# Opening input transposes cut into 128x32 column tiles, bias sums moved behind them over 128 rows, and rows 0-255 put first on SyncE's queue

## The chip, the cores and the metric

The kernel runs on one core of a Trainium2 chip. A core has five engines that work side by side and meet through semaphores: TensorE (PE in the profile), VectorE (DVE), ScalarE (ACT), GpSimd (POOL) and SyncE (SP). SP issues nothing but transfers here; ACT and POOL issue some as well, each in the order of its own instructions. The metric is the device time of one execution in microseconds, and the time of a kernel is the median of its runs.

## The reference

Six cross layers, each a product with a 416x416 matrix, a bias, a product with the first input, and a residual:

```python
B, F, D, L = 4096, 26, 16, 6
Din = min(F * D, 1024)          # 416

def reference(x0, ws, bs):      # (4096,416), (6,416,416), (6,416), all bf16
    x = x0
    for l in range(ws.shape[0]):
        x = x0 * (x @ ws[l] + bs[l]) + x
    return x
```

Since x starts as x0, the residual is folded away: the kernel keeps the running sum of `x @ ws` in PSUM, and adds to it the running sum of the biases plus 1. What a layer stores is x0 times that. So the bias is needed once, as six prefix sums for each of the 416 features.

## The kernel before

**Tiling.** The 4096 rows are four blocks of 1024 (`s`), each of two halves of 512. Features lie on partitions: three chunks of 128 (`c`, `k`, `m`) and a tail of 32. For each block and layer (`n = s * L + l`, 24 in all) TensorE does, in this order: half 0 of the three main chunks (`chunk`, `step`, 36 matmuls, each group of four filling the four column tiles of the array), the products with the 32-feature tail (`row`, L393 and L409, in two parts), the tail's own output (128x32 tiles with 256 columns), and half 1. All matmuls written through `tile_mm` are recorded at L265, whatever they compute.

**The others, in a layer.** DVE turns each PSUM chunk into the next layer's input (L537), ACT and POOL handle the tail (L595, L242, L566). TensorE waits for them by `s_xa`, `s_xb` and `s_sw`.

**The opening.** Before the first layer can run, x0 must have features on partitions. Its first block comes in four pieces of 256 rows. Piece 0 (`xin_sb[:, 0:2]`), piece 1 (`[:, 2:4]`) and piece 2 (`[:, 4:6]`) are loaded row by row and transposed by TensorE; piece 3 is transposed by a DMA (L158) that SP issues when piece 0 has landed.

- Transfers: SP issues biases (L134), piece 0 (L135), piece 2 (L136). ACT issues piece 1 (L137), the first layer's weights (L138), the tail of piece 3 (L139), then two small weight loads (L125), and only then loads its activation table.
- TensorE, in order: 40 warm-up matmuls on constants (L130, ten rounds of four column tiles); the bias sums (16 tiny matmuls over the 7 rows of `bsa_sb`, one row of ones and six of biases, against a triangle of ones `u_sb`); one more round on constants (`fill`); twelve 128x128 transposes of pieces 1 and 0 (L312) in `IN_ORDER`, whose pairs are (piece, chunk); then layer 0. In layer 0 the loop over `k` is outside: `k` 0, 1 and 2, three rounds of four matmuls each. Ahead of each `k` stands `before_a(k)`, a wait for the transposed inputs of that chunk.
- Before the second round of `k` 2 come `tail_inputs` (16 matmuls against the identity, for the tail) and `third_input` (24 of the same, for piece 2, into fp32 PSUM).
- DVE copies the bias sums out of PSUM (L506), then chunks 0 and 2 of pieces 1 and 0 (L512), later chunks 0 and 2 of piece 2 (L517). ACT copies chunk 1 (L561 and L578) and the tail (L576).

The order is written out by hand; what ties it together is the semaphores (`s_inT` counts transposed chunks, `s_inD` and `s_inA` the copies of DVE and ACT). PSUM has 8 banks. Bank 1 holds the bias sums; pieces 1 and 0 use banks 0, 5, 7 and 3, 4, 6 (`IN_BANKS[h]`); the tail uses bank 5; piece 2 uses banks 3, 6, 7.

Of the kernel before, what the change touches and what calls it, by code (L numbers as in the profile page):

```python
# [11 lines left out]
def bass_standalone__dcn_v2_cross__recsys_kernel(  # L12
# [20 lines left out]
    with ExitStack() as es:  # L33
# [20 lines left out]
        o_sb = sb("o_sb", [128, NJ, D])  # L54
        ident = sb("ident", [128, 128])
        ones_sb = sb("ones_sb", [128, 256])
        bsa_sb = sb("bsa_sb", [L + 1, D])
        u_sb = sb("u_sb", [L + 1, L])
        cb_sb = sb("cb_sb", [128, NC + 1, L], FP32)
        cq_sb = sb("cq_sb", [128, NC + 2], FP32)  # L60
        ps = es.enter_context(nc.psum_tensor("ps", [128, 8, 512], FP32))
# [34 lines left out]


        IN_BANKS = ((3, 4, 6), (0, 5, 7))
        IN_ORDER = ((1, 0), (1, 1), (1, 2), (0, 0), (0, 1), (0, 2))
        THIRD = (3, 6, 7)  # L100

        NAT_BANKS = (0, 1, 2, 6, 7, 4, 3, 5)
# [2 lines left out]
        def lane(g):  # L105
            return slice(32 * g, 32 * g + 32)
# [19 lines left out]
                wt_sb[lane(g), a:b, 0:n1 - n0], ws[a:b, DF:D, n0:n1].rearrange("l p n -> p l n")  # L126
            ).then_inc(done, 16)

        for q in range(4 * 10):
            nc.tensor.matmul(  # L130
                ps[lane(q % 4), 7, 0:256], lhsT=CONST[:, 0:32], rhs=CONST, start=True, stop=True,
                skip_group_check=True, tile_position=(0, 32 * (q % 4)),
            )
        nc.sync.dma_start(bsa_sb[1:L + 1, :], bs[:, :]).then_inc(s_bs, 16)  # L134
        nc.sync.dma_start(xin_sb[:, 0:2, :], x0_w[:, 0, :, :]).then_inc(s_xin[0], 16)  # L135
        nc.sync.dma_start(xin_sb[:, 4:6, :], x0_w[:, 2, :, :]).then_inc(s_xin[2], 16)  # L136
        nc.scalar.dma_start(xin_sb[:, 2:4, :], x0_w[:, 1, :, :]).then_inc(s_xin[1], 16)  # L137
        nc.scalar.dma_start(w_sb[:, 0, :, :], wmain(0)).then_inc(s_w[0], 16)  # L138
        nc.scalar.dma_start(xtl_sb[:, :, :], x0_v[:, 6:JS, DF:D]).then_inc(s_xtl0, 16)  # L139
        nc.gpsimd.memset(ones_sb[:, :], 1.0).then_inc(s_ones, 1)  # L140
        nc.vector.memset(wc_sb[:, :, :], 0.0).then_inc(s_zero, 1)
        nc.vector.memset(bsa_sb[0:1, :], 1.0).then_inc(s_zero, 1)

        es2 = ExitStack()
# [57 lines left out]
        @block.gpsimd  # L202
        def _(pool):
            def load_wc(i, g):
                a, b = ((0, 1), (1, L))[i]
                pool.dma_start(
                    wc_sb[lane(g), a:b, 32 * g:32 * g + 32], ws[a:b, DF:D, DF:D].rearrange("l p n -> p l n")
                ).then_inc(s_wc[i], 16)

            pool.wait_ge(s_ones, 1)  # L210
            pool.affine_select(
                out=ident[:, :], in_=ones_sb[:, 0:128], pattern=[[-1, 128]],
                compare_op=ALU.is_equal, fill=0.0, base=0, channel_multiplier=1,
            ).then_inc(s_set, 1)
            pool.affine_select(
                out=u_sb[:, :], in_=ones_sb[0:L + 1, 0:L], pattern=[[1, L]],
                compare_op=ALU.is_ge, fill=0.0, base=1, channel_multiplier=-1,
            ).then_inc(s_set, 1)
            for g in (0, 2):
                load_wt(pool, g, 0, 1, s_wtp)  # L220
            pool.wait_ge(s_zero, 1)
            for i in range(2):
                for g in (1, 3):
                    load_wc(i, g)

            for s in range(NS):
                pool.wait_ge(s_te, s + 1)
                for l in range(L):
                    n = s * L + l + 1
                    if n == NL:  # L230
                        break
                    if n == 1:
                        pool.tensor_scalar(
                            out=cq_sb[:, 0:NC + 1], in0=cb_sb[:, :, L - 1], scalar1=-1.0, scalar2=None, op0=ALU.add
                        ).then_inc(s_cq, 1)
                        pool.wait_ge(s_cq, 1)
                        pool.tensor_tensor(
                            out=cq_sb[:, NC + 1:NC + 2], in0=cq_sb[:, NC:NC + 1], in1=cb_sb[:, NC, L - 2:L - 1], op=ALU.subtract
                        ).then_inc(s_cq, 1)
                    pool.wait_ge(s_ta, n)  # L240
                    dst = xot_sb[:, s, :] if l == L - 1 else xt_sb[:, (l + 1) % 2, 0:G]
                    pool.tensor_tensor(  # L242
                        out=dst, in0=t32_sb[:, n % 2, :], in1=x0t_sb[:, s, 0:G], op=ALU.mult
                    ).then_inc(s_xt, 1)
                    if n == NL - 1:
                        pool.tensor_scalar(
                            out=xot_sb[:, s, :], in0=t32_sb[:, n % 2, :], scalar1=cq_sb[:, NC + 1:NC + 2], scalar2=None, op0=ALU.add
                        ).then_inc(s_qt, 1)
                    if l == 2 and s > 0:
                        pool.wait_ge(s_ot, 16 * s)  # L250
                        pool.tensor_copy(
                            out=o_sb[:, (s - 1) * JS:s * JS, DF:D].rearrange("p (g r) f -> p r g f", r=2),
                            in_=ot_sb[:, s - 1, :, :].rearrange("p r (g f) -> p r g f", f=DR),
                        ).then_inc(s_otc, 1)
            pool.wait_ge(s_x0n, 16)
            for i, t in enumerate(POOL_TILES):
                pool.wait_ge(s_oA, i + 1)
                pool.tensor_tensor(
                    out=o_sb[:, j0 + t, :], in0=a32_sb[:, i, :], in1=x0n_sb[:, t, :], op=ALU.mult
                ).then_inc(s_oP, 1)  # L260

        @block.tensor
        def _(pe):
# [3 lines left out]
                    skip_group_check=True, tile_position=(0, 32 * q),  # L267
                )

            def fill(n):  # L270
                for i in range(n):
                    for q in range(4):
                        tile_mm(ps[lane(q), 7, 0:256], CONST[:, 0:32], CONST, q, True)

            def tail_inputs():
                for r in range(2):
# [7 lines left out]
            def third_input():  # L284
                pe.wait_ge(s_inD, 4)
                for c in range(NC):
                    for j in range(2):
                        for q in range(4):
                            f0 = c * 128 + 32 * q
                            ins = tile_mm(  # L290
                                ps[lane(q), THIRD[c], j * 128:j * 128 + 128], xin_sb[:, 4 + j, f0:f0 + 32], ident[:, :], q, True
                            )
                    ins.then_inc(s_inT, 1)

            def bias_sums():
                pe.wait_ge(s_bs, 16)
                pe.wait_ge(s_zero, 2)
                pe.wait_ge(s_set, 2)
                for c in range(NC + 1):
                    for q in range(4):  # L300
                        f0 = c * 128 + 32 * q if c < NC else DF
                        ins = tile_mm(ps[lane(q), 1, c * 8:c * 8 + L], bsa_sb[:, f0:f0 + 32], u_sb[:, :], q, True)
                ins.then_inc(s_cbp, 1)

            bias_sums()
            fill(1)
            pe.wait_ge(s_set, 1)
            for i, (h, c) in enumerate(IN_ORDER):
                if c == 0:
                    pe.wait_ge(s_xin[h], 16)  # L310
                for j in range(2 * h, 2 * h + 2):
                    ins = pe.transpose(  # L312
                        out=psT[:, IN_BANKS[h][c], (j % 2) * 128:(j % 2 + 1) * 128],
                        in_=xin_sb[:, j, c * 128:(c + 1) * 128], identity=ident[:, :],
                    )
                ins.then_inc(s_inT, 1)

            for s in range(NS):
                for l in range(L):
# [26 lines left out]

                    def before_a(k):
                        if n == 0:
                            pe.wait_ge((s_inD, s_inA, s_inD)[k], (3, 2, 4)[k])
                        else:  # L350
                            pe.wait_ge(s_xa, NC * (n - 1) + k + 1)
                            if l == 0 and k == 0:
# [2 lines left out]
                    if n == 0:  # L355
                        pe.wait_ge(s_w[0], 16)
                        for k in range(NC):
                            before_a(k)
                            for m in range(NC):
                                if k == 0 and m == 1:  # L360
                                    pe.wait_ge(s_cb, 1)
                                if k == 2 and m == 1:
                                    pe.wait_ge(s_xin[2], 16)
                                    pe.wait_ge(s_xtl0, 16)
                                    tail_inputs()
# [136 lines left out]

        @block.vector
        def _(dve):
            dve.wait_ge(s_cbp, 1)
            dve.tensor_copy(  # L506
                out=cb_sb[:, :, :], in_=ps[:, 1, 0:8 * (NC + 1)].rearrange("p (c e) -> p c e", e=8)[:, :, 0:L],
            ).then_inc(s_cb, 1)
            for i, (h, c) in enumerate(IN_ORDER):
                if c != 1:  # L510
                    dve.wait_ge(s_inT, i + 1)
                    dve.tensor_copy(  # L512
                        out=x0T_sb[:, c, h * 256:(h + 1) * 256], in_=psT[:, IN_BANKS[h][c], 0:256]
                    ).then_inc(s_inD, 1)
            for c in (0, 2):
                dve.wait_ge(s_inT, 2 * NC + c + 1)
                dve.tensor_copy(out=x0T_sb[:, c, 512:768], in_=ps[:, THIRD[c], 0:G]).then_inc(s_inD, 1)  # L517
            dve.wait_ge(s_cb, 1)
            for s in range(NS):
                for l in range(L):  # L520
# [35 lines left out]
        def _(act):  # L556
# [18 lines left out]
            act.wait_ge(s_tp, 1)  # L575
            act.activation(out=x0t_sb[:, 0, :], in_=ps[:, 5, :], func=ACTF.Copy).then_inc(s_te, 1)  # L576
            act.wait_ge(s_inT, 2 * NC + 2)
            act.activation(out=x0T_sb[:, 1, 512:768], in_=ps[:, THIRD[1], 0:G], func=ACTF.Copy).then_inc(s_inA, 1)  # L578
            act.wait_ge(s_cb, 1)
            for s in range(NS):  # L580
                for l in range(L):
# [77 lines left out]
```

## Time and profile before

| | before |
|---|---|
| median of 6 runs | 128.37 us (127.92 to 130.24) |
| the profiled execution | 127.92 us |
| its span, first to last instruction | 126.7 us |
| PE / DVE / ACT / POOL busy | 97% / 79% / 53% / 19% |
| matmuls, DVE and ACT instructions | 2410, 154, 146 |
| DMA moved | 13.49 MB |

The span leaves out 1.2 us of the profiled execution's own time, before the first instruction and after the last. All times inside the profile count from the span's start. A line of the timeline gives start, length, engine, source line, operation, output and inputs with their sizes, how many are merged into the line, and in brackets how long the engine was idle before the first one, with what ended it. PE is the matmuls, PEld the weight loads, which overlap them.

### The profile page before, as it was taken

To read this page: it belongs to the slowest core of one execution; us is meant where nothing else is said; L and a number is where in the kernel's file an instruction comes from. 1 tells how busy PE (TensorE), PEld (TensorE's weight loads), DVE (VectorE), ACT (ScalarE), POOL (GpSimd) and SP (SyncE) were. 2 spreads that over 40 slices of the span, in tenths; PEclk is the share of its full clock that TensorE was granted. 3 is DMA by queue.
4 is the path that set the end of the run, shared out by engine and by line. 5 is a ranking of instruction groups with operands and counts; after the bars stand their busy time and mean duration, and the time that the engine had idled before them with its cause. 6 is when DMAs were issued, how large, how long until landed. Compare 5 with 4: busy or idle time off the path is not lost.

```text
span 126.7 us, 5323 instructions
## 1 busy us (share of the span) xinstructions
PE 122.9 (97%) x2410; PEld 62.1 (49%) x2410; DVE 99.8 (79%) x154; ACT 67.5 (53%) x146; POOL 24.1 (19%) x44
## 2 busy tenths in 40 slices
PE   7899999999999999999999999999999999999991
PEld 5554544545445445445445445445454454454660
DVE  2359879779779779779788798797797797797973
ACT  0646456377717456475734564574762573566830
POOL 7512202202202103012022023022021021120550
PEclk9999999999999999999999999999999999999999
DMA  3952899500009799700007679960007910530006
GB/s 112 269 134 48 230 219 170 146 0 0 5 8 157 128 155 202 270 5 5 0 5 148 128 150 207 333 189 0 5 0 47 198 35 0 172 102 5 0 30 244
DMA packets 31889, 13.49 MB, mean 107 GB/s; under 512 B 24950, under 2 KB 31868, under 8 KB 31868
## 3 DMA queue, kind: packets, MB, share of 16 engines
q1 hardware_dynamic: 30476, 12.12, 45.3%
q10 hardware_dynamic: 1200, 0.99, 2.4%
q8 instruction: 19, 0.31, 1.0%
q0 software_dynamic: 192, 0.06, 0.4%
q14 instruction: 2, 0.02, 0.0%
HBM read 3.86 MB, written 3.41 MB: 57 GB/s over the span
## 4 chain that ended last, share of the span: by engine, by line
PE 97%; DVE 1%; issue 0%
PE ps L265 82%; PE ps L393 10%; PE ps L130 2%; PE ps L449 2%; DVE x0T_sb L512 1%; PE ps L464 1%; DVE o_sb L550 0%; PE ps L488 0%; PE ps L312 0%; PE ps L409 0%; PE ps L494 0%
## 5 line engine op out<-in xcount | busy, mean ns | idle before, releaser
L537 DVE SCALAR_TENSOR_TENSOR xT_sb<-ps,cb_sb,x0T_sb 128x512 bf16<-128x512 f32 x120 | 81.0, 743 | 16.4 <-PE ps L393 16.3
L265 PE MATMUL ps<-xT_sb,w_sb 128*32 128x512 bf16 (+1 forms) x1596 | 84.2, 364 | 0.0
L265 PEld LDWEIGHTS ps<-xT_sb,w_sb 128*32 128x32 bf16 x1596 | 40.9, 97 | 37.2 <-issue 4.0
L566 ACT ACTIVATE xt_sb<-xt_sb 32x256 bf16<-32x256 bf16 x76 | 31.5, 414 | 15.7 <-POOL xt_sb L242 15.1
L595 ACT ACTIVATE t_sb<-ps,cb_sb 64x256 f32<-64x256 f32 x46 | 21.5, 468 | 31.2 <-PE ps L265 30.9
L242 POOL TENSOR_TENSOR xt_sb<-t_sb,x0t_sb 128x256 bf16<-128x256 f32 x20 | 13.4, 672 | 81.4 <-ACT t_sb L595 81.4
L265 PE MATMUL ps<-x0T_sb,w_sb 128*32 128x512 bf16 (+1 forms) x336 | 18.5, 364 | 0.3 <-DVE x0T_sb L512 0.3
L537 DVE SCALAR_TENSOR_TENSOR xo_sb<-ps,cb_sb,x0T_sb 128x512 bf16<-128x512 f32 x18 | 12.1, 743 | 2.5 <-PE ps L393 2.5
L265 PEld LDWEIGHTS ps<-x0T_sb,w_sb 128*32 128x32 bf16 x336 | 8.6, 97 | 7.8 <-issue 0.6
L393 PE MATMUL ps<-xt_sb,wt_sb 32*128 32x512 bf16 x76 | 11.5, 379 | 0.0
L614 ACT ACTIVATE x0t_sb<-x_sb 32x512 bf16<-32x512 bf16 x12 | 7.5, 626 | 0.3
L409 PE MATMUL ps<-xt_sb,wt_sb 32*128 32x512 bf16 x38 | 7.4, 385 | 0.0
L393 PE MATMUL ps<-xt_sb,wc_sb 32*128 32x256 bf16 x76 | 7.3, 268 | 0.0
L393 PEld LDWEIGHTS ps<-xt_sb,wt_sb 32*128 32x128 bf16 x76 | 2.2, 92 | 8.1 <-DVE xT_sb L537 8.1
L393 PEld LDWEIGHTS ps<-xt_sb,wc_sb 32*128 32x128 bf16 x76 | 3.8, 93 | 2.2
L242 POOL TENSOR_TENSOR xot_sb<-t_sb,x0t_sb 128x256 bf16<-128x256 f32 x3 | 2.0, 673 | 12.6 <-ACT t_sb L595 12.6
L550 DVE SCALAR_TENSOR_TENSOR o_sb<-ps,x0n_sb 128x416 bf16<-128x416 f32 x6 | 3.3, 585 | 1.0 <-PE ps L494 0.9
L570 ACT ACTIVATE xo_sb<-ps,cq_sb 128x512 bf16<-128x512 f32 x5 | 3.3, 686 | 1.1 <-PE ps L393 1.1
L130 PE MATMUL ps<-const-bfloat16-1.0 128*32 128x256 bf16 x40 | 2.3, 417 | 0.8 <-PEq L644 0.8
L561 ACT ACT_TABLE_LOAD x1 | 1.3, 1283 | 3.3 <-issue 3.3
L449 PE MATMUL ps<-w_sb,xT_sb 128*128 128x416 bf16 x12 | 2.8, 340 | 0.0
L265 PE MATMUL ps<-w_sb,xT_sb 128*32 128x416 bf16 x48 | 2.6, 339 | 0.0
(52 smaller groups left out, 38.9 us busy)
## 6 DMA issues: line engine op xcount, KB each, us to landing
out_dram<-o_sb SPq DMA_DIRECT2D x2, 832.0 KB, 5.1
w_sb<-in_ws_dram SPq DMA_DIRECT2D x5, 312.0 KB, 4.0
x0n_sb<-in_x_dram SPq DMA_DIRECT2D x1, 832.0 KB, 5.5
out_dram<-o_sb SPq DMA_DIRECT2D x1, 624.0 KB, 3.7
out_dram<-o_sb SPq DMA_DIRECT2D x3, 208.0 KB, 2.0
xin_sb<-in_x_dram SPq DMA_DIRECT2D x2, 208.0 KB, 3.2
out_dram<-o_sb ACTq DMA_DIRECT2D x2, 208.0 KB, 2.0
w_sb<-in_ws_dram ACTq DMA_DIRECT2D x1, 312.0 KB, 3.6
```

What stands on the lines that cost most here:

```text
L130: nc.tensor.matmul(ps[lane(q % 4), 7, 0:256], lhsT=CONST[:, 0:32], rhs=CONST, start=True, stop=True, skip_group_check=True, tile_position= ...
L242: pool.tensor_tensor(out=dst, in0=t32_sb[:, n % 2, :], in1=x0t_sb[:, s, 0:G], op=ALU.mult).then_inc(s_xt, 1)
L265: return pe.matmul(dst, lhsT=lhsT, rhs=rhs, start=start, stop=True, skip_group_check=True, tile_position=(0, 32 * q),)
L393: return pe.matmul(dst, lhsT=lhsT, rhs=srct[lane(g), cols], start=l == 0 and start, stop=True, skip_group_check=True, tile_position=(32 * ...
L409: pe.matmul(ps[:, NC * h + 2, :], lhsT=wt_sb[lane(g), l, 0:128], rhs=srct[lane(g), :].rearrange("p (b r) -> p b r", b=2)[:, ::-1, :], star ...
L449: pe.matmul(ps[:, NAT_BANKS[t], 0:D], lhsT=xT_sb[:, (L - 1) % 2, k, rows], rhs=w_sb[:, L - 1, k, :], start=False, stop=True, skip_group_ch ...
L537: dve.scalar_tensor_tensor(out=dst, in0=ps[:, NC * half + c, :], scalar=cb_sb[:, c, l:l + 1], in1=x0T_sb[:, c, o:o + H], op0=ALU.add, op1= ...
L550: dve.scalar_tensor_tensor(out=o_sb[:, j0 + t, :], in0=ps[:, NAT_BANKS[t], 0:D], scalar=1.0, in1=x0n_sb[:, t, :], op0=ALU.add, op1=ALU.mul ...
L566: ins = act.activation(out=buf[lane(g), G:2 * G], in_=buf[lane(g ^ 1), 0:G], func=ACTF.Copy)
L570: act.activation(out=xo_sb[:, NS - 1, c, half * H:(half + 1) * H], in_=ps[:, NC * half + c, :], func=ACTF.Identity, bias=cq_sb[:, c:c + 1] ...
L595: ins = act.activation(out=t32_sb[HALVES[h], n % 2, :], in_=tail(h), func=ACTF.Identity, bias=cb_sb[HALVES[h], NC, l:l + 1],)
L614: ins = act.activation(out=x0t_sb[lane(g), s + 1, :].rearrange("p (b n) -> p b n", b=2), in_=src[:, ::-1, :] if g % 2 else src, func=ACTF. ...
```

## The change

- The first transposes (pieces 1 and 0) are no longer twelve of 128x128 but 48 of 128x32, one per column tile (`tile_tp`). Their order changes: (piece 0, chunk 0) goes third, ahead of (piece 1, chunk 2).
- The third transposes (piece 2) become transposes too, from matmuls against the identity; so they write bf16 to PSUM, and their copies read bf16.
- The bias sums run over all 128 rows of `bsa_sb` and `u_sb`, the rows after the seventh being zero, which costs one more memset on DVE. They come after the first transposes and go to bank 5, where a transposed chunk of piece 1 lies; so they wait for ACT's first copy out of it (`s_inA`, 1). DVE copies them out after the transposed chunks.
- The warm-up has twelve rounds in place of ten; the extra round `fill` goes.
- SP issues piece 0 first, then waits for the new memset, then issues the biases and piece 2. DVE waits for the memset before it writes the row of ones.
- In layer 0, `tail_inputs` and `third_input` move up by one round, ahead of the first round of `k` 2, and the wait for the copied bias sums goes there too. The first wait of layer 0 asks for two DVE copies in place of three.

```diff
-        bsa_sb = sb("bsa_sb", [L + 1, D])
-        u_sb = sb("u_sb", [L + 1, L])
+        bsa_sb = sb("bsa_sb", [128, D])
+        u_sb = sb("u_sb", [128, L])
...
-        IN_ORDER = ((1, 0), (1, 1), (1, 2), (0, 0), (0, 1), (0, 2))
+        IN_ORDER = ((1, 0), (1, 1), (0, 0), (1, 2), (0, 1), (0, 2))
...
-        for q in range(4 * 10):
+        for q in range(4 * 12):
...
+        nc.sync.dma_start(xin_sb[:, 0:2, :], x0_w[:, 0, :, :]).then_inc(s_xin[0], 16)
+        nc.sync.wait_ge(s_zero, 1)
         nc.sync.dma_start(bsa_sb[1:L + 1, :], bs[:, :]).then_inc(s_bs, 16)
-        nc.sync.dma_start(xin_sb[:, 0:2, :], x0_w[:, 0, :, :]).then_inc(s_xin[0], 16)
         nc.sync.dma_start(xin_sb[:, 4:6, :], x0_w[:, 2, :, :]).then_inc(s_xin[2], 16)
...
+        nc.vector.memset(bsa_sb[:, :], 0.0).then_inc(s_zero, 1)
         nc.vector.memset(wc_sb[:, :, :], 0.0).then_inc(s_zero, 1)
+        nc.vector.wait_ge(s_zero, 1)
         nc.vector.memset(bsa_sb[0:1, :], 1.0).then_inc(s_zero, 1)
...
-            pool.wait_ge(s_zero, 1)
+            pool.wait_ge(s_zero, 2)
...
-            def fill(n):
-                for i in range(n):
-                    for q in range(4):
-                        tile_mm(ps[lane(q), 7, 0:256], CONST[:, 0:32], CONST, q, True)
+            def tile_tp(dst, src, q):
+                return pe.transpose(out=dst, in_=src, identity=ident[:, :], tile_position=(0, 32 * q))
...
-                            ins = tile_mm(
-                                ps[lane(q), THIRD[c], j * 128:j * 128 + 128], xin_sb[:, 4 + j, f0:f0 + 32], ident[:, :], q, True
+                            ins = tile_tp(
+                                psT[lane(q), THIRD[c], j * 128:j * 128 + 128], xin_sb[:, 4 + j, f0:f0 + 32], q
                             )
...
                 pe.wait_ge(s_bs, 16)
-                pe.wait_ge(s_zero, 2)
+                pe.wait_ge(s_zero, 3)
                 pe.wait_ge(s_set, 2)
+                pe.wait_ge(s_inA, 1)
...
-                        ins = tile_mm(ps[lane(q), 1, c * 8:c * 8 + L], bsa_sb[:, f0:f0 + 32], u_sb[:, :], q, True)
+                        ins = tile_mm(ps[lane(q), 5, c * 8:c * 8 + L], bsa_sb[:, f0:f0 + 32], u_sb[:, :], q, True)
...
-            bias_sums()
-            fill(1)
             pe.wait_ge(s_set, 1)
             for i, (h, c) in enumerate(IN_ORDER):
                 if c == 0:
                     pe.wait_ge(s_xin[h], 16)
-                for j in range(2 * h, 2 * h + 2):
-                    ins = pe.transpose(
-                        out=psT[:, IN_BANKS[h][c], (j % 2) * 128:(j % 2 + 1) * 128],
-                        in_=xin_sb[:, j, c * 128:(c + 1) * 128], identity=ident[:, :],
-                    )
+                for j in range(2):
+                    for q in range(4):
+                        f0 = c * 128 + 32 * q
+                        ins = tile_tp(
+                            psT[lane(q), IN_BANKS[h][c], j * 128:j * 128 + 128], xin_sb[:, 2 * h + j, f0:f0 + 32], q
+                        )
                 ins.then_inc(s_inT, 1)
+            bias_sums()
...
-                            pe.wait_ge((s_inD, s_inA, s_inD)[k], (3, 2, 4)[k])
+                            pe.wait_ge((s_inD, s_inA, s_inD)[k], (2, 2, 4)[k])
...
-                                if k == 0 and m == 1:
+                                if k == 2 and m == 0:
                                     pe.wait_ge(s_cb, 1)
-                                if k == 2 and m == 1:
                                     pe.wait_ge(s_xin[2], 16)
                                     pe.wait_ge(s_xtl0, 16)
                                     tail_inputs()
                                     third_input()
```

The copies follow: DVE's copy of the bias sums reads bank 5 and stands after the four copies of L512, and the copies of piece 2 (L517, L578) read the bf16 view of the banks.

More of the change, by code (lines that the diff above doesn't have):

```diff
@@ L215, in _ @@
             pool.affine_select(
-                out=u_sb[:, :], in_=ones_sb[0:L + 1, 0:L], pattern=[[1, L]],
+                out=u_sb[:, :], in_=ones_sb[:, 0:L], pattern=[[1, L]],
                 compare_op=ALU.is_ge, fill=0.0, base=1, channel_multiplier=-1,
@@ L504, in _ @@
         def _(dve):
[L505 to L508, printed above, removed]
             for i, (h, c) in enumerate(IN_ORDER):
@@ L514, in _ @@
                     ).then_inc(s_inD, 1)
+            dve.wait_ge(s_cbp, 1)
+            dve.tensor_copy(
+                out=cb_sb[:, :, :], in_=ps[:, 5, 0:8 * (NC + 1)].rearrange("p (c e) -> p c e", e=8)[:, :, 0:L],
+            ).then_inc(s_cb, 1)
             for c in (0, 2):
                 dve.wait_ge(s_inT, 2 * NC + c + 1)
-                dve.tensor_copy(out=x0T_sb[:, c, 512:768], in_=ps[:, THIRD[c], 0:G]).then_inc(s_inD, 1)
+                dve.tensor_copy(out=x0T_sb[:, c, 512:768], in_=psT[:, THIRD[c], 0:G]).then_inc(s_inD, 1)
             dve.wait_ge(s_cb, 1)
@@ L577, in _ @@
             act.wait_ge(s_inT, 2 * NC + 2)
-            act.activation(out=x0T_sb[:, 1, 512:768], in_=ps[:, THIRD[1], 0:G], func=ACTF.Copy).then_inc(s_inA, 1)
+            act.activation(out=x0T_sb[:, 1, 512:768], in_=psT[:, THIRD[1], 0:G], func=ACTF.Copy).then_inc(s_inA, 1)
             act.wait_ge(s_cb, 1)
```

## The prediction

> **What bounds the kernel now.** I read the page's shares first, then the chain that ended last cut to the opening, then the timeline of the first 10 us. The shares:
>
> ```profile
> PE 122.9 (97%) x2410; PEld 62.1 (49%) x2410; DVE 99.8 (79%) x154; ACT 67.5 (53%) x146; POOL 24.1 (19%) x44
> ```
>
> TensorE works all the time. The chain (start, length, what) says where it doesn't:
>
> ```profile
> 0.83 2.32 PE ps L130 x36
> ...
> 4.06 0.78 DVE x0T_sb L512 x3
> 4.83 0.14 issue
> 4.97 2.69 PE ps L265 x76
> 7.65 0.36 PE ps L393
> ...
> 8.32 4.33 PE ps L265 x84
> 12.65 0.32 PE ps L393
> ```
>
> From 8.3 us on one layer follows another every 4.87 us (12.65 to 17.52, and so on) with TensorE as the only engine in the chain, and no diff line touches that part. So the change is worth exactly what it shifts the moment when that rhythm begins, which is the weight load at 8.25. The timeline of the opening:
>
> ```profile
> 3.27 1.28 ACT L561 ACT_TABLE_LOAD   x1 [3.27 <-issue]
> 3.62 1.00 PE L312 MATMUL ps<-ident,xin_sb 128*128 128x128 bf16 x12
> 4.06 0.96 DVE L512 COPY x0T_sb<-ps 128x256 bf16<-128x256 bf16 x4 [0.44 <-PE ps L312]
> 4.56 0.66 ACT L561 ACTIVATE x0T_sb<-ps 128x256 bf16<-128x256 bf16 x2
> 4.94 1.23 PEld L265 LDWEIGHTS ps<-x0T_sb,w_sb 128*32 128x32 bf16 x28 [0.48 <-DMA w_sb<-in_ws_dram]
> 4.97 1.70 PE L265 MATMUL ps<-x0T_sb,w_sb 128*32 128x512 bf16 x28 [0.34 <-DVE x0T_sb L512]
> 7.61 0.09 PEld L393 LDWEIGHTS ps<-x0t_sb,wt_sb 32*128 32x128 bf16 x1 [0.46 <-DVE x0T_sb L517]
> 8.25 1.74 PEld L265 LDWEIGHTS ps<-x0T_sb,w_sb 128*32 128x32 bf16 x44 [0.21 <-DMA x0T_sb<-in_x_dram]
> ```
>
> Four things to see. ACT's first copy can't start before 4.55, when its table load ends. Layer 0 starts at 4.97, held by the third DVE copy (ends 4.82) and by the first weights (issued 1.22, 3.6 us to landing: 4.82). The tail products wait until 7.61 for ACT's tail copy, which ends at 7.55. The 0.21 at 8.25 is hardly a DMA wait: in a full layer the step from the second tail part to the next 128x32 matmuls is 12.81 to 13.12, 0.31; here it is 7.92 to 8.25, 0.33.
>
> **The change part by part**, on this execution's own time, 127.92 (span 126.7), which lies 0.45 below the median.
>
> *Warm-up.* Ten rounds take 0.213 each (0.83 to the last start at 2.74), so twelve are issued by 0.83 + 12 x 0.213 = 3.39. Before, bias sums and fill kept TensorE until 3.29 + 0.21 = 3.50, and the transposes began at 3.62. Now they can begin at about 3.5 if piece 1 is there (issued 0.80, 2.6 to landing: 3.4). Gain at this point 0.1; it is lost again below.
>
> *48 tiled transposes.* The trace has no transpose in a column tile; its nearest row is the 40 matmuls of 128x32 against the identity, 6.47 to 7.03: 0.56, or 0.056 per round of four. The full transposes are spaced the same: 0.107 each until 4.03, about 0.055 after, where their recorded length falls from 314 ns to 219. So TensorE's speed doubles at 4.03, though the granted clock is printed as full throughout. Taken side by side as in that row, 12 rounds cost what 12 full ones did, and end about 4.4 (4.8 if the speed rises late). If the four column tiles didn't overlap, each round would cost four times as much; that is a rival. Below nothing isn't possible: the rounds stream the same 128 columns.
>
> *Bias sums, moved.* This is the term that decides. They wait for `s_inA` 1, ACT's first copy, and that starts when the table load ends (4.55) and takes 379 to 383 ns: 4.94. Neither earlier transposes nor earlier rows help, as nothing on ACT moves. ACT's end to TensorE's load takes 0.06 (7.55 to 7.61), so: load 5.00, first matmul 5.03. Sixteen of them went from 3.09 to 3.36, the last 0.16 long, so 0.11 from first start to last, 0.12 with one step. More rows don't add columns to stream. Layer 0 then starts at about 5.17, not 4.97: **+0.20**. Queued behind that wait on TensorE is all of layer 0. [...]
>
> *Waits of layer 0 that become earlier.* `s_inD` 2 in place of 3, (0, 0) third, DVE's bias copy out of the way: now met at about 4.65 instead of 4.82. Worth nothing, as 5.17 covers it by 0.5. The first weights (4.82) are covered by 0.35. `k` 1 needs ACT's second copy (4.84 + 0.38 = 5.22); it starts at 5.17 + 3 x 0.215 = 5.82.
>
> *Tail and third inputs one round earlier.* They began after seven rounds, at 6.47; now after six: 5.17 + 6 x 0.215 = 6.46. So this gives back the 0.20. They wait for piece 2 (issued 1.67, 3.7 to landing: 5.37), for the tail of piece 3 (issued 1.74, 4.5: 6.24; cover 0.22), and for the bias copy (5.15 + 0.2 to write + 0.2 for the copy: 5.6; cover 0.9). The 40 tiles end at 6.46 + 0.56 = 7.02, and the three rounds of `k` 2 at 7.02 + 0.645 = 7.67, where two ended at 7.46.
>
> *The stall at 7.61.* ACT's tail copy still ends at 7.55, since its inputs come at the same time. Before, TensorE had ended at 7.46 and started at 7.64. Now it arrives at 7.67, with no wait. What is late next is TensorE itself: from the 128x32 to the 32x128 products takes 0.11 (12.47, the end of the round started at 12.26, to 12.58), so 7.78. Second part: 0.23 later (12.58 to 12.81), 8.01; ACT's copy of piece 2 (ends 7.82) and DVE's (bf16 now, 0.29 each in place of 0.42) are in time. Then 0.31: **8.32, against 8.25: +0.07**. The earlier, cheaper bf16 copies (2 x 0.13 on DVE) are worth nothing: 7.88 is the latest that any copy allows, against 8.01.
>
> *SP's queue.* Piece 0 is issued at 0.80 instead of 1.25, so L158 at about 3.5 instead of 3.91; its piece landed 4.1 after issue (8.01), now 7.6 to 8.0, wanted at 8.32: no gain, no loss. The biases wait for a memset of 128x416 zeros; the row of 480 words took 0.46, so 0.2 as words (208) or 0.4 as elements; the biases leave at 1.2 to 1.4, piece 2 0.1 to 0.3 later (landing 5.5 to 5.7, cover 0.8). The weights of the next layer follow L158 (L166 at 5.24, 4.0 to landing, needed past 10). POOL's wait for the second memset (about 1.65) is covered by its own issues until 2.84.
>
> *Sum.* Layer 0 +0.20; one round moved behind the inputs -0.215, and run there +0.215; from there the waits that no longer bind: 0.18 to the tail products becomes 0.11 (-0.07), 0.28 to their second part becomes 0.23 (-0.05), 0.33 to the rhythm becomes 0.31 (-0.02); sum +0.06, or +0.07 by the times above. Profiled 127.92 + 0.07 = 127.99; on the median 128.37 + 0.07 = 128.44. A change under 0.5%, 0.64 us, is about what can't be told from none here.
>
> [...]
>
> **Rivals.**
> - *Column tiles don't overlap in transposes* (slower). From 3.55, 48 one by one: 4 until 4.03, 44 x 0.055 = 2.4, end 6.45 with bias sums at 6.5 and layer 0 at about 6.6 (+1.4); piece 2 24 x 0.055 = 1.32 in place of 0.33 (+1.0). 128.44 + 2.4 = 130.8. It decides once the first transposes end past 5.0. For it: the form is not in the trace. Against: 128x32 matmuls do overlap.
> - *Transfers slip.* Pieces 0 and 1 now start together, and from 2.5 to 4.5 us the DMA moved 372 GB/s, so it is full. If all of piece 0 (0.21 MB) went ahead of ACT's weights: 0.21/0.372 = 0.57; weights 5.39, layer 0 5.45 (+0.28); tail of piece 3 at 6.81 with the rest, +0.15 more: 128.9. Against: the same bytes in all.
> - *TensorE's speed rises late* in most runs: 128.44 + 1.1 = 129.5. For it: the runs before spread to 130.24.
> - *The extra plain rounds make it rise early always*: the 0.45 between the profiled run and the median goes, 128.0, at the edge of faster.
>
> **How the numbers follow.** Forecast 0.52; transfers slip 0.16; late rise 0.12; always early 0.12; no overlap 0.08. Same: the forecast, half the slips, two thirds of always early and a little of the rest: 0.65. Slower: no overlap, late rise, some slips: 0.26. Faster: 0.09. The range leaves out no overlap, and reaches from always early with noise (127.8) to late rise (129.6); the forecast's own is 128.1 to 128.8.
>
> **What would show it.** Right: bias matmuls at about 5.03, straight after ACT's first copy, and TensorE idle ahead of them; layer 0 at 5.15 to 5.2; no idle before L393; rhythm from 8.3. Wrong: transposes spaced over 0.1 per round at full speed; main rounds spaced 0.43 in place of 0.215; a DMA as releaser of layer 0 or of the tail inputs; ACT's table load at another time, since everything hangs on it.

## The result, and the profile after

Over 29 runs the changed kernel takes a median of 129.65 us (128.19 to 131.27), the kernel before 128.47 us over 66 runs (127.90 to 130.89). Compared run against run the ratio is 1.0064, with a 95% interval of 1.0046 to 1.0082: slower by about 0.8 us. I had forecast no change (128.44, chance 0.65) and slower with 0.26. The ratio applied to the 128.37 of the forecast gives 129.19, inside the range of 127.8 to 129.6; the median of all runs lies just above its upper end. The ratio leaves out the slow runs, those over 1.5% above the fastest of their kernel (six of the 29), and the profiled execution of the changed kernel, 130.17 us with a span of 128.9, is one of them, so the waits below are larger than those of a median run. The 29 runs are not alike: 8 lie between 128.19 and 128.78, as the kernel before does, and 21 from 129.08 up, so the loss is not the same in every execution.

The shares first (same view as before):

```profile
PE 123.5 (96%) x2450; PEld 62.7 (49%) x2450; DVE 99.8 (77%) x155; ACT 67.6 (52%) x146; POOL 24.0 (19%) x44
```

The span grew by 2.2 us and TensorE's busy time by 0.6, its 40 more records. So there is new idle time on TensorE. The chain that ended last, cut to the opening (start, length, what):

```profile
1.73 6.76 DMA xtl_sb<-in_x_dram
8.49 0.14 issue
8.63 0.42 PE ps L268 x16
...
10.03 0.32 PE ps L394
...
10.57 4.33 PE ps L268 x84
...
15.44 4.33 PE ps L268 x84
```

The rhythm is what it was: 10.57 to 15.44 is 4.87 us. It begins 2.25 later than before (8.32 there). The chain now runs through a transfer, the tail of piece 3, which lands at 8.49 in place of 6.24. The transfers concerned, with their KB and the us from issue to landing (the tail and the transposing DMA; the first two lines before, the others after):

```profile
xtl_sb<-in_x_dram ACTq DMA_DIRECT2D x1, 16.0 KB, 4.5
x0T_sb<-in_x_dram SPq DMA_TRANSPOSE x1, 4.1
xtl_sb<-in_x_dram ACTq DMA_DIRECT2D x1, 16.0 KB, 6.8
x0T_sb<-in_x_dram SPq DMA_TRANSPOSE x1, 6.2
```

The timeline shows where TensorE lost what:

```profile
3.81 1.30 SPq L161 DMA_TRANSPOSE x0T_sb<-in_x_dram  x1
4.13 1.47 PE L274 MATMUL ps<-ident,xin_sb 128*32 128x128 bf16 x48 [0.54 <-DMA xin_sb<-in_x_dram]
4.79 0.38 ACT L562 ACTIVATE x0T_sb<-ps 128x256 bf16<-128x256 bf16 x1 [0.25 <-PE ps L274]
5.36 0.32 PE L268 MATMUL ps<-u_sb,bsa_sb 128*32 128x6 bf16 x16
5.71 1.48 PE L268 MATMUL ps<-x0T_sb,w_sb 128*32 128x512 bf16 x24
8.63 0.24 PE L268 MATMUL ps<-ident,xin_sb 128*32 128x128 bf16 x3 [1.44 <-DMA xtl_sb<-in_x_dram]
...
10.50 0.45 PEld L268 LDWEIGHTS ps<-x0T_sb,w_sb 128*32 128x32 bf16 x20 [0.21 <-issue]
```

The first transposes wait for piece 1 (4.0 to land, 3.4 before), so ACT's first copy is at 4.79 and not straight after its table load; layer 0 starts at 5.71, just after the first weights land (1.24 + 4.4 = 5.64; 4.82 before); then comes the idle stretch for the tail. From the tail inputs on, every step has the length that was forecast: tail inputs at 8.63, tail products at 9.96, rhythm at 10.50, where the forecast had 6.46, 7.78 and 8.32. The transposing DMA (L161), 4.1 us to landing before, takes 6.2 here and lands at 10.0. So even with the tail in time the rhythm could not have begun before 10.0, and the tail's lateness costs at most some 0.5 of the 2.25 us; the chain names the tail because, with TensorE held up by it, the transposing DMA was there first.

The tail's late landing is not late data. The DMA queues (packets, MB, share of 16 engines; q10 is ACT's queue, q1 is SP's, q0 POOL's), from 5.25 to 5.5 us and from 5.5 to 8.4:

```profile
q0 software_dynamic: 26, 0.01, 38.0%
q1 hardware_dynamic: 39, 0.01, 36.2%
q10 hardware_dynamic: 15, 0.00, 4.6%
```

```profile
GB/s 55 152 148 185 215 219 212 141 60 39 92 74 117 205 275 523 301 236 178 180 80 34 57 69 0 0 11 23 0 41 30 7 11 7 16 0 23 0 11 11
...
q1 hardware_dynamic: 853, 0.27, 103.5%
q8 instruction: 1, 0.02, 2.2%
q0 software_dynamic: 41, 0.01, 2.1%
```

ACT's queue moves its last 15 packets before 5.5 and none after; the tail counts as landed 3 us later. Nearly all that moves in between is SP's queue, with the transposing DMA and behind it the next layer's weights (L169), and in the last 1.2 us before 8.4 that is at most 41 GB/s. The tail's semaphore counts to 16, and the trace has the time of each increment: 15 of them come between 5.28 and 5.67 (before: 5.25 to 5.64), and the last alone at 8.49 (before: 6.20). One part of sixteen is late, not the transfer.

### The profile page after: what moved, and what is told of

It is laid out like the page before. It is cut to its first block, busy times and chain, and to the rows that moved or that the text cites. A ratio compares the mean times of both kernels' runs of the same rounds, so it can differ in the third digit from the quotient of the medians.

```text
span 128.9 us, 5406 instructions
## 1 busy us (share of the span) xinstructions
PE 123.5 (96%) x2450; PEld 62.7 (49%) x2450; DVE 99.8 (77%) x155; ACT 67.6 (52%) x146; POOL 24.0 (19%) x44
## 3 DMA queue, kind: packets, MB, share of 16 engines
HBM read 3.86 MB, written 3.41 MB: 56 GB/s over the span
## 4 chain that ended last, share of the span: by engine, by line
PE 91%; DMA 5%; ACTq 1%; DVE 0%; issue 0%
PE ps L268 79%; PE ps L394 10%; DMA xtl_sb<-in_x_dram 5%; PE ps L450 2%; PE ps L465 1%; DVE o_sb L551 0%; PE ps L489 0%; ACTq L139 0%; ACTq L138 0%; PE ps L274 0%; PE ps L410 0%; PE ps L495 0%
## 5 line engine op out<-in xcount | busy, mean ns | idle before, releaser
L130 PE MATMUL ps<-const-bfloat16-1.0 128*32 128x256 bf16 x48 | 2.8, 418 | 0.8 <-PEq L645 0.8
L509 DVE COPY x0T_sb<-ps 128x256 bf16<-128x256 bf16 x4 | 1.1, 291 | 2.8 <-PE ps L274 2.5
L518 DVE COPY x0T_sb<-ps 128x256 bf16<-128x256 bf16 x2 | 0.5, 290 | 3.2 <-PE ps L274 3.2
```

Source lines behind the costliest of these rows:

```text
L130: nc.tensor.matmul(ps[lane(q % 4), 7, 0:256], lhsT=CONST[:, 0:32], rhs=CONST, start=True, stop=True, skip_group_check=True, tile_position= ...
```

## The experiments

The theory after the traces: SP's new order lets piece 0 share the DMA with ACT's loads from the start; those come late and run into the transposing DMA. The rival theory: the parts on TensorE (tiled transposes, bias sums behind ACT's copy) cost the time.

**SP's order alone, on the kernel before.**

```diff
-        nc.sync.dma_start(bsa_sb[1:L + 1, :], bs[:, :]).then_inc(s_bs, 16)
         nc.sync.dma_start(xin_sb[:, 0:2, :], x0_w[:, 0, :, :]).then_inc(s_xin[0], 16)
+        nc.sync.dma_start(bsa_sb[1:L + 1, :], bs[:, :]).then_inc(s_bs, 16)
```

> The kernel before with one edit: SP issues piece 0 first and the biases second. Transfers theory (piece 0, 0.45 us earlier, shares the DMA with piece 1 and the first weights from the start, so ACT's queue is served later and the tail of piece 3 behind it later still): piece 1 lands near 4.0 instead of 3.4, the weights near 5.5 instead of 4.8, the tail of piece 3 at 7.5 or later instead of 6.2, and the time is 0.4 to 1% over the kernel before. TensorE theory (the tiled transposes and the bias sums behind ACT's copy cost the time): no difference, within 0.2%.

Measured: 130.24, ratio 1.014 (1.0103 to 1.0176). The order alone costs more than the whole change. The bias sums before, then in this run, and this run's chain:

```profile
3.09 0.27 PE L265 MATMUL ps<-u_sb,bsa_sb 7*32 7x6 bf16 x16
4.11 0.28 PE L265 MATMUL ps<-u_sb,bsa_sb 7*32 7x6 bf16 x16 [0.95 <-DMA bsa_sb<-in_bs_dram]
```

```profile
1.24 4.95 DMA w_sb<-in_ws_dram
6.18 0.04 issue
6.23 4.56 PE ps L265 x56
```

Two waits: the biases now hold up the head of TensorE's queue, where the bias sums still stand (4.11, before 3.09), and the weights land at 6.18. The tail, which I had expected at 7.5 or later, landed at 6.4, and the transposing DMA took 4.3 us: in this run the order costs its time by other transfers than in the changed kernel's trace. The move of the bias sums behind the transposes may pay back a part of what the order costs; no run moves them alone. The 4.56 us for 56 records shows a third loss: rounds spaced 0.43 (0.215 in layer 0 of the kernel before), TensorE at half speed, which it had not left yet (its transposes still took 314 ns at 5.8).

**SP's order undone, the rest of the change kept.**

```diff
-        nc.sync.dma_start(xin_sb[:, 0:2, :], x0_w[:, 0, :, :]).then_inc(s_xin[0], 16)
-        nc.sync.wait_ge(s_zero, 1)
         nc.sync.dma_start(bsa_sb[1:L + 1, :], bs[:, :]).then_inc(s_bs, 16)
+        nc.sync.dma_start(xin_sb[:, 0:2, :], x0_w[:, 0, :, :]).then_inc(s_xin[0], 16)
...
-        bsa_sb = sb("bsa_sb", [128, D])
-        u_sb = sb("u_sb", [128, L])
+        bsa_sb = sb("bsa_sb", [L + 1, D])
+        u_sb = sb("u_sb", [L + 1, L])
...
```

The memset over the 128 rows and the waits for it go as well.

> The changed kernel with SP's old order (biases, piece 0, piece 2, no wait for a memset) and therefore with the bias tile of 7 rows again; tiled transposes, bias sums behind them in bank 5 and twelve warm-up rounds stay. Transfers theory: the tail of piece 3 lands near 6.2 again, layer 0 starts near 5.2, and the time is within 0.2% of the kernel before. TensorE theory: 0.5 to 0.7% slower than before, as the changed kernel.

Measured: 128.46 against 128.39, ratio 1.000 (0.9981 to 1.002). The loss is gone, though the tiled transposes, the moved bias sums and the longer warm-up are all there: the rival theory falls. The 128 rows, which left with the order, are no cost as sums: the sixteen matmuls take 0.26 us here with 7 rows, and 0.26 with 128 in the run with the tail on SP below. Timeline:

```profile
4.57 0.66 ACT L559 ACTIVATE x0T_sb<-ps 128x256 bf16<-128x256 bf16 x2
5.10 0.26 PE L265 MATMUL ps<-u_sb,bsa_sb 7*32 7x6 bf16 x16 [0.16 <-ACT x0T_sb L559]
5.29 1.48 PE L265 MATMUL ps<-x0T_sb,w_sb 128*32 128x512 bf16 x24
...
7.90 0.09 PEld L391 LDWEIGHTS ps<-x0t_sb,wt_sb 32*128 32x128 bf16 x1 [0.42 <-DVE x0T_sb L515]
...
8.45 0.45 PEld L265 LDWEIGHTS ps<-x0T_sb,w_sb 128*32 128x32 bf16 x20 [0.21 <-issue]
```

This is the opening that the forecast had worked out: table load, ACT's copy, bias sums, layer 0, and the rhythm from 8.45 (8.25 before, 8.32 forecast). The transposing DMA lands 3.9 us after issue.

**The transposing DMA held back until the tail has landed** (changed kernel).

```diff
             sp.wait_ge(s_xin[0], 16)
+            sp.wait_ge(s_xtl0, 16)
```

> The changed kernel, with SP also waiting for the tail of piece 3 before it issues the transposing DMA. If the packets of the transposing DMA crowd the tail out: the tail lands by 6.5 (within 1.0 us of the first weights), but the transposed piece then lands near 10.5 and TensorE waits for it, some 2 us, 1.5% over before. If the row loads alone are the cause: the tail still lands at 7.5 or later, and the time is 2.5% or more over before.

Measured: 128.88, ratio 1.0047 (1.0026 to 1.0067). The chain, and the queues from 5.25 to 5.5 us:

```profile
1.73 4.13 DMA xtl_sb<-in_x_dram
5.86 0.02 issue
...
5.94 3.02 DMA x0T_sb<-in_x_dram
8.96 0.04 issue
9.00 3.09 PE ps L269 x57
```

```profile
q0 software_dynamic: 34, 0.01, 65.1%
q10 hardware_dynamic: 11, 0.00, 4.0%
```

ACT's queue ends in the same quarter of a microsecond as in the changed kernel, but now the tail counts as landed at 5.86 instead of 8.49. So it is the transposing DMA in flight that held it in the execution traced above. I had the price wrong: issued after the tail's landing, that DMA takes 3.0 us and not 4.1, so it lands at 8.96. TensorE would have been ready for it at 8.73 (second tail part at 8.42, and 0.31). The rhythm begins at 9.00 in place of 8.25; 0.27 of that is this wait, and the rest was lost before layer 0, which starts at 5.58. These 0.75 us of one execution stand beside the 0.6 us of the ratio.

**The tail on SP, behind piece 2** (changed kernel).

```diff
         nc.sync.dma_start(xin_sb[:, 4:6, :], x0_w[:, 2, :, :]).then_inc(s_xin[2], 16)
+        nc.sync.dma_start(xtl_sb[:, :, :], x0_v[:, 6:JS, DF:D]).then_inc(s_xtl0, 16)
...
-        nc.scalar.dma_start(xtl_sb[:, :, :], x0_v[:, 6:JS, DF:D]).then_inc(s_xtl0, 16)
```

> The changed kernel with the tail of piece 3 issued by SP behind piece 2 instead of by ACT behind the first weights. Transfers theory: the tail lands by 6.5, the 1.4 us wait for it goes; ACT has one issue less, so its table load begins 0.5 us earlier (2.75); what is left is the weights' landing near 5.6, and the time is 0.2% over to 0.3% under before. TensorE theory: as the changed kernel, 0.5% over before.

Measured: 130.51, ratio 1.0109 (1.0056 to 1.0163); my expectation falls. The chain has the tail again:

```profile
2.05 5.64 DMA xtl_sb<-in_x_dram
```

The table load did begin at 2.74, but the tail still landed at 7.69, although it stands ahead of the transposing DMA in its own queue, and that DMA took 5.4 us. So the tail's place in ACT's queue is not the point. To be unfinished when the transposing DMA starts is not enough either: in the kernel before and with SP's order alone the tail was under way at that moment, too (3.91 and 3.86), and landed at 6.24 and 6.4.

**The tail ahead of the first weights**, on the changed kernel and on the kernel before.

```diff
+        nc.scalar.dma_start(xtl_sb[:, :, :], x0_v[:, 6:JS, DF:D]).then_inc(s_xtl0, 16)
         nc.scalar.dma_start(w_sb[:, 0, :, :], wmain(0)).then_inc(s_w[0], 16)
-        nc.scalar.dma_start(xtl_sb[:, :, :], x0_v[:, 6:JS, DF:D]).then_inc(s_xtl0, 16)
```

> The changed kernel with the tail of piece 3 ahead of the first weights in ACT's queue. If the tail is late because the transposing DMA runs by the time its turn comes: it lands by 4.6, the stall before the tail inputs goes, and what is left is layer 0 waiting for the weights at 5.6 to 5.8: 0.3 to 0.4% over before, with a narrower spread than the changed kernel. If small rows of 64 bytes are slow wherever they stand: it lands past 6, and nothing is gained.

> The kernel before with the same edit. The tail lands at 6.24 there and is wanted at 6.46, so in the profiled run there is nothing to gain: same within 0.2%, if the weights still land by 4.9. If the tail is late in a part of the runs of before, too, these get shorter: 0.1 to 0.3% faster.

Measured: 130.09 on the changed kernel, ratio 1.0083 (1.005 to 1.0116); 131.37 against 128.53 on the kernel before, over 6 runs (no ratio is on record for it). The tail lands at 4.4 and 4.0, as hoped, and both are slower: now the weights stand behind it. Chain and groups of the kernel before with this edit:

```profile
1.74 4.90 DMA w_sb<-in_ws_dram
6.64 0.04 issue
6.68 4.56 PE ps L265 x74
```

```profile
L265 PE MATMUL ps<-x0T_sb,w_sb 128*32 128x512 bf16 x28 | 3.2, 630 | 1.6 <-DMA w_sb<-in_ws_dram 1.6
```

The weights slip from 4.82 to 6.64 in this execution (in the changed kernel's traces only from 5.64 to 5.84) with one small transfer ahead of them, and the mean of 630 ns per matmul (379 before) says that TensorE ran at half speed after the wait, as its transposes had (287 to 314 ns throughout).

**Piece 0 0.37 us later** (changed kernel).

```diff
-        nc.sync.dma_start(xin_sb[:, 0:2, :], x0_w[:, 0, :, :]).then_inc(s_xin[0], 16)
         nc.sync.wait_ge(s_zero, 1)
+        nc.sync.dma_start(xin_sb[:, 0:2, :], x0_w[:, 0, :, :]).then_inc(s_xin[0], 16)
```

> The changed kernel with one line moved: SP waits for the memset first (over at about 1.14) and issues piece 0 then, near 1.2, about where the kernel before has it; the biases follow, piece 2 behind them near 2.05. If the start of piece 0 at 0.80 is what makes piece 1, the weights and the tail late: piece 1 lands near 3.4 to 3.6, weights by 5.1, tail by 6.6, time within 0.2% of before. If it is the biases behind piece 0, or anything on TensorE: 0.5 to 0.7% slower, as the changed kernel.

Measured: 128.82, ratio 1.0039 (1.0019 to 1.0058), between the two forecasts, and its interval overlaps that of the changed kernel. TensorE no longer waits for pieces 0 to 2, the weights or the tail, but the chain shows another late one:

```profile
1.17 2.74 DMA xin_sb<-in_x_dram
3.91 0.01 issue
3.93 5.01 DMA x0T_sb<-in_x_dram
8.94 0.04 issue
8.98 4.17 PE ps L268 x77
```

The transposing DMA needs 5.0 us, and TensorE waits for its piece until 8.98.

**Biases last on SP**, with piece 0 later and with piece 0 at 0.80 (changed kernel).

```diff
 # first kernel
+        nc.sync.wait_ge(s_zero, 1)
         nc.sync.dma_start(xin_sb[:, 0:2, :], x0_w[:, 0, :, :]).then_inc(s_xin[0], 16)
+        nc.sync.dma_start(xin_sb[:, 4:6, :], x0_w[:, 2, :, :]).then_inc(s_xin[2], 16)
-        nc.sync.wait_ge(s_zero, 1)
         nc.sync.dma_start(bsa_sb[1:L + 1, :], bs[:, :]).then_inc(s_bs, 16)
-        nc.sync.dma_start(xin_sb[:, 4:6, :], x0_w[:, 2, :, :]).then_inc(s_xin[2], 16)
 # second kernel: piece 0, piece 2, the wait, the biases
```

> The changed kernel with SP's issues in another order: wait for the memset, piece 0 (near 1.2), piece 2 (1.6), biases last (2.0). This gives the two pieces the starts that they had before. If starts of the large pieces are all that matters: the same as before within 0.2%, or a little slower where the bias sums wait for the biases (they landed 3.4 us after issue in the run with piece 0 later, so near 5.4 here, 0.3 after ACT's copy: at most 0.2% over). If the biases must be the first thing on the queue for another reason: 0.4 to 0.6% slower, as with piece 0 alone later.

> The changed kernel with piece 0 at 0.80 and piece 2 at 1.25, both 0.4 us earlier than before, biases last. If earlier starts of SP's pieces push ACT's weights and tail behind the start of the transposing DMA: slower than the changed kernel, 0.7 to 1.2% over before, with weights past 5.5. If the order against the biases is what counts: as the run with biases last and piece 0 later.

Measured: 129.62, ratio 1.0042 (1.0015 to 1.0069), and 129.81, ratio 1.0079 (1.0051 to 1.0106). I had expected earlier pieces to be worse; the two intervals overlap, so that is not shown. In both traces it is the biases that hold TensorE (landing at 6.31 and 5.67, where they were issued at 2.09 and 1.72), and in the second the transposed piece as well (9.1).

**A candidate**: SP's old order, tail ahead of the weights, ACT's two small weight loads on SP, so that the table load comes 1 us earlier; and the same without the tail's move.

```diff
 # on the kernel with SP's order undone, both
-            for g in (1, 3):
-                load_wt(act, g, 0, 1, s_wt[0])
...
+            for g in (1, 3):
+                load_wt(sp, g, 0, 1, s_wt[0])
             sp.wait_ge(s_xin[0], 16)
```

> The changed kernel with SP's old order and 7-row bias tile, the tail of piece 3 ahead of the first weights, and ACT's two small weight loads on SP behind piece 2, so that ACT's table load begins 1 us earlier (2.3) and its first copy near 4.1 to 4.3 instead of 4.56. By the chain through ACT's copy, bias sums at 4.6 to 4.7 and layer 0 at the weights' landing, 4.85 to 4.95 instead of 5.2: 0.2% faster than before. If the weights land later for it, nothing is gained.

> The changed kernel with SP's old order and the 7-row bias tile, and ACT's two small weight loads issued by SP behind piece 2; the tail of piece 3 stays behind the first weights. ACT's table load begins near 2.3, its first copy near 4.1, bias sums near 4.7, layer 0 at the weights (4.85): 0.1 to 0.3% faster than before, if the chain through ACT's copy is what holds layer 0. If the two loads in SP's queue delay the transposing DMA or the weights, the same or slower.

Measured: 132.12, ratio 1.0199 (1.0139 to 1.0259), and 128.81, ratio 1.0024 (1.0006 to 1.0041). Both expectations fall. In the second, table load and copy came at 2.24 and 4.22 as planned, but the tail landed at 7.1 and the transposing DMA took 5.2 us. The move of the two small loads is all that parts this kernel from the one with SP's order undone, where that DMA took 3.9. No version beat the kernel before.

**Fifteen warm-up rounds** (changed kernel).

```diff
-        for q in range(4 * 12):
+        for q in range(4 * 15):
```

> The changed kernel with fifteen warm-up rounds in place of twelve. They are issued by 0.83 + 15 x 0.213 = 4.03, and TensorE waited for piece 1 until 4.13 in the changed kernel, so they cost nothing. If the idle time between 3.4 and 4.1 is what makes TensorE's speed rise late in a part of the runs (transposes at 314 ns, rounds spaced 0.43 in the slower kernels tried), the runs past 130 become rare and the median falls to 0.2 to 0.4% over before. If the late transfers are all, it stays at 0.6 to 0.9% over before with the same spread.

Measured: 129.86 over 6 runs (129.41 to 130.73), ratio 1.0123 (1.0088 to 1.0158). TensorE's speed rose during the transposes (mean of the first 48: 275 ns, 311 in the changed kernel), and the time didn't fall. The chain:

```profile
0.80 3.02 DMA xin_sb<-in_x_dram
3.82 0.02 issue
3.83 6.20 DMA x0T_sb<-in_x_dram
10.04 0.04 issue
10.08 3.09 PE ps L268 x57
```

The tail is in time here (the tail inputs start at 6.81), and the rhythm begins at 10.08 all the same: the transposing DMA is the bound by itself, 6.2 us. A late rise of the speed is not what holds the median; whether it makes some of the longest runs of the changed kernel is not shown, and in its trace layer 0 runs at full speed (24 matmuls in 1.48 us). The changed kernel was not run beside this one, so whether 1.0123 is really worse than 1.0064 stays open.

## Why the prediction was right or wrong

- **The step that failed** is "SP's queue": "now 7.6 to 8.0, wanted at 8.32: no gain, no loss". In the traced execution the transposing DMA was issued at 3.81, not 3.5, took 6.2 us and landed at 10.0. Its companions failed with it: "if piece 1 is there (issued 0.80, 2.6 to landing: 3.4)" and the covers of 0.35 and 0.22 for the weights and the tail. I took each landing as issue plus the duration of the trace before. But these durations belong to one order of the queues: with piece 0 at 0.80 piece 1 took 3.2, the weights 4.4, the tail 6.8. With SP's order undone the ratio is 1.000, so the whole loss lies in this step and its companions.
- **That the time still fell into the range is in part luck.** Its upper end of 129.6 stood there for a late rise of TensorE's speed, not for a transposing DMA that lands 2 us late, and the forecast itself was no change, where the interval of the ratio lies above 1. The chances do not add up either: forecast 0.52, half the slips 0.08 and two thirds of always early 0.08 are 0.68 for the same time, and I wrote 0.65.
- **The rival "Transfers slip"** (0.16) named the right place and the wrong size: 0.43 (0.28 and 0.15) from bytes over bandwidth. Bytes were not what it took: the tail's data had left by 5.5, and the tail counted as landed at 8.49, by one increment of sixteen, with the transposing DMA in flight, and at 5.86 with that DMA held back. How it holds an increment back, no run shows.
- **The forecast's own mechanism held.** The run with SP's order undone is its test. ACT's copy 4.57 to 4.96 (4.56 to 4.94 forecast), bias sums 5.10 (5.03), layer 0 5.29 (5.17), tail inputs 6.59 (6.46), tail products 7.90 (7.78), rhythm 8.45 (8.32). The terms that were mis-sized are the hop from ACT's copy to the sums, 0.14 and not 0.09, and the sums themselves, 0.19 to the next start and not 0.12 to 0.14.
- **Tiled transposes** overlap: 48 in 1.47 us at half speed, 0.85 at full speed in the run with the tail on SP. The rival without overlap falls.
- **TensorE's late rise** is real: half-speed rounds, with matmuls of 512 columns at up to 634 or 635 ns in place of 379, stand in the traces of four of the slower kernels (order alone, tail first on the kernel before, the first candidate, biases last with piece 0 later). The +1.1 that I gave it, and with it the upper end of the range, was my estimate, and no run shows it. With SP's order alone the seven rounds ahead of the tail inputs took 2.96 us (6.23 to 9.19) where the kernel before took 1.50 (4.97 to 6.47), so 1.46 more. With SP's order undone there was no such loss: all 48 transposes ran at half speed (1.47 us), and layer 0 behind them at full speed (24 matmuls in 1.48 us). More warm-up didn't bring the time back (129.86 us with fifteen rounds).
- **The cheaper copies and earlier waits** were forecast to be worth nothing. DVE's copies of piece 2 do take 0.29 each, and the kernel with all of TensorE's parts is at 1.000; alone they were not measured.

**What stays open**: why the transposing DMA takes 3.0 us in one run, 3.9 to 4.7 in five, and 4.9 to 6.2 in the others. No order of issues sorts these: it took 4.0 with piece 0 first and the tail ahead of the weights, and 5.2 with the biases first and two small loads more on SP.

One candidate stands in the traces and was not tested. Queue q8, whose kind the views give as "instruction", moves one packet of 16 KB from 6.62 to 7.65 us in the changed kernel, in the middle of the transposing DMA; in the kernel before it comes at 8.85, after that DMA has landed. Straight behind it, from 7.63 to 7.99, 13 of the DMA's packets of 256 bytes start one after another, and sixteen packets of the next weights that began between 6.90 and 7.74 all end between 8.44 and 8.49, with the tail's last increment. From 7.0 to 8.6 us 104 packets start in all. The run with fifteen rounds, the other one with 6.2 us, is like it: the packet of q8 starts between 6.5 and 7, and 77 packets start from 7.0 to 8.6; in the kernel before and in every other run these are 416 or more. So the DMA moved the least there in the two runs where the transposing DMA took longest. That the instruction load makes it do so is not shown: no run moved the load by itself, and with SP's order undone it comes between 6.5 and 7, too, and the transposing DMA took 3.9.

## What to carry to other kernels

A transfer's time to landing was not the transfer's own: in these runs the same tail of 16 KB took 2.8 to 6.8 us from issue to landing, and the same transposing DMA 3.0 to 6.2. When a diff reorders a queue at a time when the DMA is full (here 372 GB/s at a share of 1.07 from 2.5 to 4.5 us in the kernel before), a landing from the trace before is no cover unless the margin is wider than such a spread; here margins of 0.2 to 0.35 fell, and landings moved by up to 2.25 us. And the parts of a change are not judged one by one: SP's order alone cost 1.4%, the whole change with the same order first 0.64%, the rest without it nothing.

## What the hardware showed unexpectedly

- A small transfer whose last packet had moved by 5.5 us counted as landed at 8.49 with a transposing DMA in flight, and at 5.86 without. Fifteen of its sixteen increments had come by 5.67.
- The same transposing DMA of 256 rows took from 3.0 us (issued after the tail's landing) to 6.2 us to land. In the changed kernel's execution with 6.2 us the core's DMA moved at most 41 GB/s for 1.2 us, from 7.2 to 8.4, ahead of the landing at 10.0.
- With one transfer of 16 KB in rows of 64 bytes ahead of them, the first weights (312 KB) landed at 6.64 in place of 4.82 us on the kernel before, and at 5.84 in place of 5.64 on the changed one.
- Sixteen matmuls of six columns in four column tiles start 7 ns apart on average (0.11 us from the first start to the last in the kernel before).
